# Centring first: a transposed copy without the deviation for two pairs of tiles, and one queue for the first loads

## The chip, the cores and the metric

The kernel runs on one core of a Trainium2 chip. The metric is the device time of one execution in microseconds (us). The kernel before takes 153.9 us (median of 3 runs, 153.81 to 154.15). The profiled execution, from which all durations below come, took 153.96 us, of which 152.2 us lie between its first and its last instruction.

## The reference

x is 2048 x 448 (bf16). Each row is normalised, and two branches and x itself are added up:

```
xn  = (x - mean) / sqrt(var + eps)
q, k, v = xn @ wqkv                      # 16 heads of 28
pq, pk  = q @ w_phi, k @ w_phi           # one 28 x 28 matrix for each head
phi     = [softmax(p), softmax(-p)]      # for pq and pk, 56 features
kv, z   = sum over s of phi_k * v, of phi_k
o       = (phi_q @ kv) / (phi_q @ z + 1e-6)
h       = xn @ w1 + b1                   # 448 -> 1792
out     = x + o @ wo + (h * tanh(softplus(h))) @ w2
```

Normalising a row is a subtraction and a product with one number, rstd = 1/sqrt(var + eps). Products with a matrix are linear, so xn @ W = rstd * ((x - mean) @ W), row by row.

## The kernel before, in words

The 2048 rows are 16 tiles t of 128 rows; two tiles make a pair u = t // 2. A pair's normalised rows (xn, 2 x 448 wide) are turned (transposed) into xnT, seven chunks of 128 features. The odd 64 features of the two tiles share the middle chunk, which is why most products run as two halves of 64 rows that TensorE (PE) executes at once; 14 such halves make one step for a pair.

The order is written out by hand in one string, ORDER (L147). Each word is a step, and each engine gets its instructions in the order in which the steps stand there. The words, with u, t or fc (one of 14 columns of 128 of w1) as number:

- `lx`: load of x tiles; `lkm`, `lkt`, `lvm`: the key and value columns of wqkv, rows 0 to 383 and the last 64 rows, loaded twice, into partitions 0 to 63 and 64 to 127; `lqT`: the query columns by a transposing DMA; `l1m`, `l1t`: w1. The last letter is the queue (s for SP, a for ACT).
- `z12`: twelve products of zeros on PE at the start. `st`: mean and variance of a tile (on DVE, or on ACT by two sums). `rs`, `rt`: rstd (on POOL, or on ACT by Ln and Exp). `xn`: normalising. `xt`: turning a pair, by PE and copies out of PSUM (b, a, d) or by a transposing DMA on SP's queue (m).
- `wtk0`, `wtk1`, `wmk0`, `wmk1`: the key columns are turned on PE, copied to SBUF, multiplied by w_phi and copied into Wpk, so that pk = xn @ Wpk in one step. `qd`, `wmq0`, `wmq1`: the same for queries, from the four `lqT` loads, into Wpq.
- `v`, `k`, `q` with A, B, H: the three parts of a pair's step (14 halves) for values, keys and queries. Then ACT or DVE copies the values (L509, L511), and ACT writes exp(+p) and exp(-p), one instruction of 896 columns for each sign over both tiles (L609, L682).
- `kn`, `kc`: sum of the key exponentials over a head (DVE), reciprocal, product (POOL, L621 or L633). `kv`: the sum over s (L650), which needs all of these. `e`: the query exponentials turned by DMA. `nd`: numerator and denominator (L723). `f`: h for half of the rows and one fc, then ACT's Mish (L703). `wo`, `g`: the two output products (L845, L828). `sto`, `stt`: stores.

PSUM has eight banks; v, k, q and f each take a pair of banks and give it back when the last copy or activation out of it has run. The pair taken is the one that was used longest ago, so PE can be at most four such steps ahead of the engine that empties them.

Waits are put down once the order is fixed: each instruction waits for the last writers and readers of what it touches.

Of the kernel before, what the change touches and what calls it, by code (L numbers as in the profile page):

```python
# [146 lines left out]
ORDER = """  # L147
pi lx1.2a pw table lx0.1s lx4.6a lx2.4a zero st1d lpa st5a st0d st4d st2d rs0p lvma rs2p lx6.8a xn0a xn1d lkms xn5p
lkts xn4p lx8.10s lbs st3d z12 wtk0a rt2a wtk1d xt0b lqT3 rt3a wmk0d wmk1a pp b1 xt2b xn2d st8d lqT1 lqT2 lqT0 xn3d
st9d k0B lx12.14a k2B xt1m st7d qd lx10.12s lx14.16a rt8p pv st6d k0A k0H st12d rt9p k2H v2Ba v0Ba v2Ha v2Aa v0Aa rs3p  # L150
st13d xn6d l1ts st15d xn7d xt3m v0Ha wmq1a wmq0a k2A rt12p rt13p xn13p xn12p st10d xt6m xn8p st14d k1A v1Bd k1B st11d
q2B k1H rs5p v1Ad q1H q2H v1Hd rt14a q1B xn10d q2A xn9d xn14d rt15p pk xt4m q0A q1A q0B k3B xn15d xt7m v6Ba k3H q0H
v6Aa xn11p kn0.1 k6H v6Ha k3A kn0.0 xt5m kn1.1 l1ms k6A v3Ad kc3 k6B v3Hd k7A v3Bd k7H v4Hd kn6.0 e3 v4Ad k7B v4Bd k4B
v7Ba k4H k4A e2 k5B kn7.1 v7Aa kn7.0 q4H k5A v7Ha kc2 e0 k5H q4A e5 f0.0B q4B f0.0H v5Bd f0.0A e9 f0.8H f0.8A v5Ad
kn5.0 f0.3B f0.8B v5Hd f0.3A e1 f0.4B f0.3H e8 q3B f0.4A f0.5A f0.4H f0.5H f0.2H f0.2A kn1.0 f0.5B kn4.1 q5H e4 q5A
f0.2B q3H kn6.1 loa q7B q5B q7A q7H kn5.1 kn4.0 kv2 kv6 ep kv1 kv0 kv5 kv7 kv4 kv3 q3A f1.0B kvz f0.9A e10 f1.0A f1.0H
e14 f0.9H e15 f0.6A f0.9B f0.7B f0.6H nd0 f0.7A f0.6B f0.11H f0.11A f0.7H f0.10B nd3 f0.11B f0.12A f0.10A e11 e6
f0.10H nd1 f0.12H e7 ot0m f0.1B f0.12B f0.1A f0.1H q6A q6H f1.13H nd2 q6B f1.5A f1.13A f1.4A f1.13B f1.5H f1.1H f1.1A
f1.4B f1.1B f1.5B f1.6A f1.6H e12 f1.4H ot1m f1.11A f1.6B f1.11B nd4 f1.12H f1.11H l2s f1.12A f0.13B f1.12B f1.7A nd5
f1.7H f0.13H f0.13A f1.2H f1.7B ot2m f1.2A nd7 wo0H f1.2B wo1B wo0A wo1A nd6 ot3m wo1H wo0B nd10 g2 g7 g3 g1 g0 nd12  # L160
e13 f1.10A f1.10H f1.9A f1.9H wo3B f1.10B nd13 f1.9B wo3A wo3H f1.8B ot6m f1.3H nd11 f1.3A ot5m g6 g5 f1.8H nd15 f1.8A
wo2H f1.3B sto1 wo2B nd14 nd9 wo2A nd8 g4 sto3 g14 g9 sto2 g12 ot7m g8 ot4m g13 wo7H wo4B wo7A wo5A wo6A wo5H wo6H
wo4A wob wo5B wo4H wo6B wo7B sto0 g10 g11 g15 sto6 stt14 sto5 sto4 stt15
"""
# [815 lines left out]
```

## Time and profile before

| | |
|---|---|
| median of 3 runs | 153.9 us |
| profiled execution | 153.96 us |
| its span, first to last instruction | 152.2 us |
| outside the span | 1.76 us |
| PE busy | 144.6 us (95%) |
| DVE busy | 101.1 us (66%) |
| ACT busy | 75.7 us (50%) |
| POOL busy | 44.3 us (29%) |

A row of the timeline or of the chain begins with its start and its length in us. A row of the groups gives the count, the busy time, the mean length of one in ns, and the idle time before. Back-to-back instructions of one engine overlap by their ends, so n of them take less than n times the mean length; the time from one start to the next is what a queue of them costs.

### The profile page before, as it was taken

The page shows a single profiled execution, that of the slowest core. Times are in us where ns is not written, and L with a number is a line of the kernel's source. Part 1 is how long each engine was busy: PE and PEld are TensorE (multiplying, and loading weights), DVE is VectorE, ACT ScalarE, POOL GpSimd, SP SyncE. Part 2 cuts the span into 40 slices and gives each one's busy share as a digit, 9 for nine tenths or more (in the row PEclk, how much of TensorE's full clock was granted, in tenths as well). Part 3 has the DMA queues.
Part 4 walks back from the last instruction along what each step waited for, and adds up shares of the span by engine and source line. Part 5 has one row for each costly group of instructions (what it writes and reads, how often), then busy time and mean ns, then how long its engine had stood idle before and what let it go on. Part 6 is the DMA issues. An engine that isn't in the chain of part 4 may idle for free.

```text
span 152.2 us, 3611 instructions
## 1 busy us (share of the span) xinstructions
PE 144.6 (95%) x1541; PEld 76.1 (50%) x1541; DVE 101.1 (66%) x223; ACT 75.7 (50%) x90; POOL 44.3 (29%) x65
## 2 busy tenths in 40 slices
PE   3978999989999979999999999999999999999993
PEld 1454545445444574445344455554544554559552
DVE  0699989599969903599606999535995999200721
ACT  3485999995995699778997730000500400000000
POOL 3385688969999950000000000000000000000000
PEclk9999999999999999999999999999999999999999
DMA  5995964989967243994399260500035000540204
GB/s 123 288 260 147 174 143 93 131 268 262 101 137 138 76 139 73 180 197 41 60 149 321 86 65 14 119 0 0 2 65 151 30 4 0 121 121 4 87 4 151
DMA packets 40436, 17.22 MB, mean 113 GB/s; under 512 B 34020, under 2 KB 39908, under 8 KB 40420
## 3 DMA queue, kind: packets, MB, share of 16 engines
q1 hardware_dynamic: 37548, 14.46, 46.9%
q10 hardware_dynamic: 2872, 2.53, 5.6%
q8 instruction: 12, 0.20, 0.5%
q14 instruction: 4, 0.03, 0.1%
HBM read 7.02 MB, written 1.84 MB: 58 GB/s over the span
## 4 chain that ended last, share of the span: by engine, by line
PE 78%; ACT 12%; DMA 4%; DVE 3%; issue 1%; ACTq 0%
PE PS L429 38%; PE PS L828 28%; PE PS L845 7%; DMA x_all<-in_A_x_dram 4%; ACT actT L609 3%; PE PS L723 2%; PE PS L650 2%; ACT actT L682 2%; ACT v_all L509 2%; DVE Sk L627 1%; ACT Wpq L509 1%; ACT Eq L682 1%; DVE v_all L511 1%; ACT Eq L509 1%; ACT Wpk L509 1%
## 5 line engine op out<-in xcount | busy, mean ns | idle before, releaser
L703 ACT ACTIVATE actT<-PS,b1T 128x1024 bf16<-128x1024 f32 x28 | 30.2, 1112 | 33.1 <-PE PS L429 33.0
L429 PE MATMUL PS<-xnT,W 64*128 64x512 bf16 x392 | 46.2, 376 | 0.0
L828 PE MATMUL PS<-W,actT 128*128 128x448 bf16 (+1 forms) x224 | 42.7, 351 | 0.0
L828 PEld LDWEIGHTS PS<-W,actT 128*128 128x128 bf16 x224 | 21.5, 98 | 20.3 <-issue 0.7
L429 PEld LDWEIGHTS PS<-xnT,W 64*128 64x128 bf16 x392 | 18.1, 94 | 21.0 <-ACT actT L703 0.4
L793 DVE TENSOR_TENSOR x_all<-PS,x_all 128x448 bf16<-128x448 f32 (+1 forms) x16 | 9.5, 616 | 20.3 <-PE PS L845 10.3
L621 POOL TENSOR_TENSOR actT<-actT,rSk 128x896 bf16<-128x896 bf16 x12 | 20.0, 1699 | 0.0
L609 ACT ACTIVATE actT<-PS 128x896 bf16<-128x896 f32 x16 | 13.7, 950 | 3.7 <-DVE stats L466 1.8
L429 PE MATMUL PS<-Wkv,xnT 64*128 64x448 bf16 x112 | 13.6, 349 | 0.6 <-DVE v_all L511 0.6
L429 PE MATMUL PS<-Wpk,xnT 64*128 64x448 bf16 x112 | 13.3, 349 | 0.5 <-ACT Wpk L509 0.5
L429 PE MATMUL PS<-Wpq,xnT 64*128 64x448 bf16 x112 | 12.7, 350 | 0.0
L466 DVE BATCH_NORM_STATS2 stats<-x_all 128x6 f32<-128x448 bf16 x15 | 9.2, 614 | 5.2 <-DMA x_all<-in_A_x_dram 5.2
L617 DVE TENSOR_REDUCE Sk<-actT 128x32 f32<-128x896 bf16 x12 | 12.5, 1043 | 0.0
L738 DVE COPY Sq<-PS 128x16 f32<-128x16 f32 x32 | 4.0, 167 | 12.5 <-PE PS L723 12.2
L749 DVE TENSOR_TENSOR xn<-v_all,rden 128x448 bf16<-128x448 f32 x16 | 10.0, 625 | 1.3 <-DMA Wkv<-xn 0.8
L746 DVE TENSOR_TENSOR v_all<-v_all 128x464 f32<-128x464 f32 x16 | 10.3, 642 | 0.6
L742 DVE TENSOR_TENSOR v_all<-PS,Sq 128x464 f32<-128x464 f32 x16 | 10.3, 642 | 0.5
L744 DVE TENSOR_TENSOR v_all<-PS,Sq 128x464 f32<-128x464 f32 x16 | 10.1, 630 | 0.0
L429 PEld LDWEIGHTS PS<-Wkv,xnT 64*128 64x128 bf16 x112 | 5.4, 94 | 6.0 <-DVE v_all L511 1.0
L682 ACT ACTIVATE actT<-PS 128x896 bf16<-128x896 f32 x10 | 8.4, 926 | 0.0
L429 PEld LDWEIGHTS PS<-Wpk,xnT 64*128 64x128 bf16 x112 | 5.3, 94 | 5.5 <-ACT Wpk L509 0.6
L429 PEld LDWEIGHTS PS<-Wpq,xnT 64*128 64x128 bf16 x112 | 5.1, 94 | 5.4 <-ACT actT L609 0.5
(85 smaller groups left out, 137.7 us busy)
## 6 DMA issues: line engine op xcount, KB each, us to landing
W<-in_B_w_dram SPq DMA_DIRECT2D x1, 1568.0 KB, 8.0
out_dram<-x_all SPq DMA_DIRECT2D x7, 224.0 KB, 2.2
W<-in_B_w_dram SPq DMA_DIRECT2D x1, 1344.0 KB, 7.2
x_all<-in_A_x_dram ACTq DMA_DIRECT2D x5, 224.0 KB, 4.1
Wo<-in_A_wo_dram ACTq DMA_DIRECT2D x2, 336.0 KB, 3.6
x_all<-in_A_x_dram SPq DMA_DIRECT2D x2, 224.0 KB, 4.9
W<-in_B_w_dram SPq DMA_DIRECT2D x2, 224.0 KB, 4.0
Wkv<-in_A_wqkv_dram SPq DMA_DIRECT2D x1, 336.0 KB, 4.2
```

What stands on the lines that cost most here:

```text
L429: ins = e.matmul(o, lhs(c, k), rhs(c, k), start=first and n == at[par][0], stop=last and n == at[par][-1])
L609: op("ACT", lambda e, s=s: e.activation(E_of(u)[:, s, :, :], two(b, D), ACT.Exp, scale=1.0 if s == 0 else -1.0), r=[pb(b), pb(b + 1)], w=[ ...
L617: op("DVE", lambda e: e.tensor_reduce(Sk[u][:, s, :], Eh(), AX.X, ALU.add), r=[("E", u, s)], w=[("Sk", u, s)], tag=f"Sk{u}.{s}")
L621: op("POOL", lambda e: e.tensor_tensor(Eh(), Eh(), ap_on(rSk[u][:, s, 0:1], [[1, 2 * H], [0, DH]]), ALU.mult), r=[("E", u, s), ("rSk", u, ...
L682: op("ACT", lambda e, s=s: e.activation(Eq_of(u)[:, :, s, :].rearrange("p i (h n) -> p i h n", n=64)[:, :, :, 0:QP], two(b, D).rearrange(" ...
L703: op("ACT", lambda e: e.activation(actT[:, q, fc, :], bank(b, 2), ACT.Mish, bias=b1T[:, fc:fc + 1]), r=[("b1T",), pb(b), pb(b + 1)], w=[(" ...
L742: op("DVE", lambda e: e.tensor_tensor(tv(t1[i]), num(0), sx(1), ALU.mult), r=[pb(b), pb(b + 1), ("Sq", i, 1)], w=[("t1", i)], tag=f"ta{t}")
L744: op("DVE", lambda e: e.tensor_tensor(tv(t2), num(1), sx(0), ALU.mult), r=[pb(b), pb(b + 1), ("Sq", i, 0)], w=[("t2",)], tag=f"tb{t}")
L746: op("DVE", lambda e: e.tensor_tensor(t1[i], t1[i], t2, ALU.add), r=[("t1", i), ("t2",)], w=[("t1", i)], tag=f"tc{t}")
L749: op("DVE", lambda e: e.tensor_tensor(o_sb[(t // 2) % 2][:, t % 2, :].rearrange("p (h d) -> p h d", d=DH), t1[i][:, :, 0:DH], ap_on(rden[i ...
L828: ins = e.matmul(bank(b)[:, 0:width(t)], act_of(fc, t), W2[:, fc, 0:width(t)], start=first and fc == 0, stop=last and fc == FC - 1)
L845: ins = e.matmul(bank(b)[:, 0:w], oT_of(u)[lo:hi, cc * P:(cc + 1) * P], Wo[lo:hi, cc, 0:w], start=first and n == at[par][0], stop=last and ...
```

## The change

For two pairs (u = 0 and u = 2) the turned copy is made of x - mean, before rstd is known. It lies in the space of EqT, which is free at that time. `xc` centres a tile (DVE or POOL), `ct` turns the pair on PE, with one ACT copy of 896 columns out of PSUM. The v, k and q steps of these pairs read this copy, and rstd goes in where the results leave PSUM: as the per-partition scale of a copy (values) or of Exp (keys, queries; nrstd = -rstd for the second sign). rstd differs between the two tiles of a pair, so each such instruction covers one tile, 448 columns. The same two pairs are still normalised and turned the old way (by DMA) for the f steps. The last 64 rows of the key columns are loaded once, and the four transposes that read them run as two halves each. All loads of the first stage go through SP's queue, w_phi and b1 through ACT's. `z12` is `z7`. The whole ORDER string is another.

```diff
-pi lx1.2a pw table lx0.1s lx4.6a lx2.4a zero st1d lpa st5a st0d st4d st2d rs0p lvma rs2p lx6.8a xn0a xn1d lkms xn5p
...
+lx1.2s zero pw lx0.1s lx4.6s st1d lkms xc1d lkts pi pp table lpa lx2.4s st0a xc0d lba st5d rt1p lvts xc5p st4d z7 rt0a
...
+    nrstd = sb("nrstd", [P, 8], FP32)
...
+    XR, XC = (15, 14, 13, 12), (11, 10, 9, 8)
+
+    def flat_of(t):
+        return EqT[:, t, :, :].rearrange("p c n -> p (c n)")[:, 0:7 * P]
+
+    def xR(u):
+        return flat_of(XR[u]).rearrange("p (c n) -> p c n", n=P)
...
+    def load_kv_tail(i, eng):
+        lo, hi = HALF[i]
+        dst, src = (Wv, A_wqkv[384:448, 2 * D:3 * D]) if i else (Wkv, A_wqkv[384:448, D:3 * D])
+        dma(eng, lambda e: e.dma_start(dst[lo:hi, 3, :], src), w=[("Wt", i)], tag=f"ldWt{i}")
...
-                    ins = e.transpose(oT(c)[:, g, :], Wk[:, 2 * h + c, g * GP:(g + 1) * GP], ident[:])
+                    for lo, hi in HALF if h and c else ((0, P),):
+                        ins = e.transpose(oT(c)[:, g, lo:hi], Wk[0:hi - lo, 2 * h + c, g * GP:(g + 1) * GP],
+                                          ident[0:hi - lo, 0:hi - lo])
...
+    def center(t, eng):
+        u = t // 2
+        for n, (lo, hi, at) in enumerate([(0, D, 0)] if t % 2 == 0 else [(384, D, D), (0, 384, D + 64)]):
+            src, dst = x_all[:, t, lo:hi], flat_of(XC[u])[:, at:at + hi - lo]
+            op(eng, lambda e, src=src, dst=dst: e.tensor_scalar(dst, src, mv[:, t, 0:1], 0.0, op0=ALU.subtract, op1=ALU.add),
+               r=[("x", t), ("mean", t)], w=[("xc", u, t % 2, n), ("EqT", XC[u])], tag=f"xc{t}.{n}")
...
+        pe(lambda e: transpose7(e, b, flat_of(XC[u])), r, [pb(b)], f"cT{u}")
+        evac(eng, lambda: flat_of(XR[u]), lambda: bank16(b)[:, 0:7 * P], [pb(b)], [("xR", u), ("xRU", u)] + home, f"cTE{u}")
...
+    def v_early(u, part, eng):
...
+                if eng == "ACT":
+                    op("ACT", lambda e, dst=dst, src=src, t=t: e.mul(dst, src, rstd[:, t:t + 1]), r=r, w=w, tag=f"vs{u}.{i}")
...
+    def k_early(u, part):
+        def then(b):
+            for s in range(2):
+                for i in range(2):
+                    t = 2 * u + i
+                    op("ACT", lambda e, s=s, i=i, t=t: e.activation(E_of(u)[:, s, i, :], bank(b + i)[:, 0:D], ACT.Exp,
+                                                                    scale=sign_rstd(t, s)),
...
+    def q_early(u, part):
```

On PE, the start of the program, before (L504 turns normalised pairs, L547 and L571 are the key columns' `wtk` and `wmk`, L429 the v, k, q steps):

```order
L370 MATMUL PS<-zeros 128x512 x12
L547 MATMUL PS<-ident,Wkv 112x128 x16
L504 MATMUL PS<-ident,xn 128x128 x7
L571 MATMUL PS<-Wbd,Eq 128x112 x16
L695 MATMUL PS<-ident,b_rows 128x14
L504 MATMUL PS<-ident,xn 128x128 x7
L429 MATMUL PS<-Wpk,xnT 128x448 x22
L429 MATMUL PS<-Wkv,xnT 128x448 x28
L571 MATMUL PS<-Wbd,WqT 128x112 x16
```

Now (the lines have moved: L524, L568, L593, L449):

```order
L390 MATMUL PS<-zeros 128x512 x7
L524 MATMUL PS<-ident,EqT 128x128 x7
L568 MATMUL PS<-ident,Wkv 112x128 x12
L568 MATMUL PS<-ident,Wkv 112x64 x8
L593 MATMUL PS<-Wbd,Eq 128x112 x16
L786 MATMUL PS<-ident,b_rows 128x14
L524 MATMUL PS<-ident,EqT 128x128 x7
L449 MATMUL PS<-Wkv,EqT 128x448 x6
L449 MATMUL PS<-Wpk,EqT 128x448 x6
```

The first pair is turned ahead of the key columns, from the centred copy, and the first v half-step stands ahead of the first k half-step.

On ACT, from the first turned pair on, before (L509 copies out of PSUM, L609 key exponentials):

```order
L509 ACTIVATE xnT<-PS 128x384
L478 ACTIVATE lnv<-mv,eps_col 128x1
L480 ACTIVATE rstd<-lnv 128x1
L509 ACTIVATE Wpk<-PS 128x896
L509 ACTIVATE xnT<-PS 128x384
L273 DMA x_all<-in_A_x_dram 128x896 x2
L609 ACTIVATE actT<-PS 128x896 x2
L509 ACTIVATE v_all<-PS 128x32x28 x2
L509 ACTIVATE Wpq<-PS 128x2x4x56 x4
L609 ACTIVATE actT<-PS 128x896 x4
```

Now (L529 copies, L662 values with rstd, L673 key exponentials with rstd or -rstd):

```order
L529 ACTIVATE EqT<-PS 128x896
L529 ACTIVATE Wpk<-PS 128x896 x2
L529 ACTIVATE EqT<-PS 128x896
L498 ACTIVATE lnv<-mv,eps_col 128x1
L500 ACTIVATE rstd<-lnv 128x1
L515 ACTIVATE xn<-x_all,shift,rstd 128x448
L662 ACTIVATE v_all<-PS,rstd 128x16x28 x2
L673 ACTIVATE actT<-PS,rstd 128x448 x2
L673 ACTIVATE actT<-PS,nrstd 128x448 x2
L498 ACTIVATE lnv<-mv,eps_col 128x1
L500 ACTIVATE rstd<-lnv 128x1
L529 ACTIVATE Wpq<-PS 128x2x4x56 x2
```

ACT copies both turned pairs and both halves of Wpk whole, and has four instructions of 448 columns where a key step had two of 896.

On SP's queue, the first loads, before:

```order
L273 DMA x_all<-in_A_x_dram 128x448
L276 DMA Wkv<-in_A_wqkv_dram 128x3x448
L281 DMA Wkv<-in_A_wqkv_dram 64x896 x2
L273 DMA x_all<-in_A_x_dram 128x896
L303 DMA b_rows<-in_B_b_dram 14x128
L285 DMA_TRANSPOSE WqT<-in_A_wqkv_dram 128x448 x4
L516 DMA_TRANSPOSE xnT<-xn 128x7x128
L273 DMA x_all<-in_A_x_dram 128x896
L281 DMA W<-in_B_w_dram 64x1792 x2
```

Now:

```order
L287 DMA x_all<-in_A_x_dram 128x448 x2
L287 DMA x_all<-in_A_x_dram 128x896
L290 DMA Wkv<-in_A_wqkv_dram 128x3x448
L301 DMA Wkv<-in_A_wqkv_dram 64x896
L287 DMA x_all<-in_A_x_dram 128x896
L301 DMA Wkv<-in_A_wqkv_dram 64x448
L290 DMA Wkv<-in_A_wqkv_dram 128x3x448
L287 DMA x_all<-in_A_x_dram 128x896 x2
L304 DMA_TRANSPOSE WqT<-in_A_wqkv_dram 128x448 x4
L536 DMA_TRANSPOSE xnT<-xn 128x7x128
L287 DMA x_all<-in_A_x_dram 128x896
L287 DMA x_all<-in_A_x_dram 128x1792
```

Five loads that stood in ACT's queue now stand ahead of the transposing loads for the queries, and the last two loads of x stand behind the first transposed pair, which waits for DVE.

More of the change, by code (lines that the diff above doesn't have):

```diff
@@ L153 @@
[L153 to L162, printed above, removed]
@@ L244, in _kernel, with early_of @@
                  "Wp1": [("Wp", 1, h, c) for h in range(2) for c in range(2)]}
+    XR, XC = (15, 14, 13, 12), (11, 10, 9, 8)
[3 more added lines that the diff above has]
+        return flat_of(XR[u]).rearrange("p (c n) -> p c n", n=P)
+    def early_of(t):
+        return [(n, XR.index(t)) for n in ("xR", "xRU")] if t in XR else \
+            [("xc", XC.index(t), i, n) for i in range(2) for n in range(2 if i else 1)] if t in XC else []
     def oT_of(u):
@@ L292, in rows_of @@
     def rows_of(name):
-        return [(name, 0), ("Wt", 0), ("Wt", 1)] if name in ("Wk", "Wv") else [(name, i) for i in range(3)]
+        return [(name, 0), ("Wt", 0)] + ([("Wt", 1)] if name == "Wv" else []) if name in ("Wk", "Wv") else \
+            [(name, i) for i in range(3)]
     def load_phi(eng):
@@ new lines, in k_early, with then @@
+    def k_early(u, part):
+        def then(b):
+            for s in range(2):
+                for i in range(2):
+                    t = 2 * u + i
+                    op("ACT", lambda e, s=s, i=i, t=t: e.activation(E_of(u)[:, s, i, :], bank(b + i)[:, 0:D], ACT.Exp,
+                                                                    scale=sign_rstd(t, s)),
+                       r=[pb(b + i), ("rstd", t), ("nr", u)], w=[("E", u, s)] if i else [("Eh", u, s)], tag=f"exkc{u}.{s}.{i}")
+        pair_part(f"k{u}", part, tok_works(u, Wp[1], True),
+                  x_res(u, True) + [("Wp", 1, h, c) for h in range(2) for c in range(2)], then)
@@ new lines, in q_early, with then @@
+    def q_early(u, part):
+        def then(b):
+            for s in range(2):
+                for i in range(2):
+                    t = 2 * u + i
+                    op("ACT", lambda e, s=s, i=i, t=t: e.activation(
+                        Eq_of(u)[:, i, s, :].rearrange("p (h n) -> p h n", n=64)[:, :, 0:QP],
+                        bank(b + i)[:, 0:D].rearrange("p (h n) -> p h n", n=QP), ACT.Exp, scale=sign_rstd(t, s)),
+                       r=[pb(b + i), ("Eqp", u % 3), ("rstd", t), ("nr", u)], w=[("Eq", u % 3, s)],
+                       tag=f"exqc{u}.{s}.{i}")
+        pair_part(f"q{u}", part, tok_works(u, Wp[0], True), x_res(u, True) + [("Wp", 0, c) for c in range(4)], then)
@@ L903, in _kernel @@
                 add(f"f{q}.{fc}{part}", ffn1, q, fc, part)
+    for u in range(4):
+        add(f"nr{u}", minus_rstd, u)
+        for eng, c in (("ACT", "a"), ("DVE", "d"), ("both", "b")):
+            add(f"ct{u}{c}", center_T, u, eng)
+        for part in "ABH":
+            add(f"v{u}{part}e", v_early, u, part, "ACT")
+            add(f"v{u}{part}f", v_early, u, part, "DVE")
+            add(f"k{u}{part}c", k_early, u, part)
+            add(f"q{u}{part}c", q_early, u, part)
+        for t in (2 * u, 2 * u + 1):
+            add(f"xc{t}d", center, t, "DVE")
+            add(f"xc{t}p", center, t, "POOL")
     add("kvz", kvz)
```

62 lines of the change are left out of this document (50 added, 12 removed).

## The prediction

> **What bounds the kernel now.** I read the page first, then the chain of waits, busy time by stretches of the span, and the timeline of the first 60 us.
>
> ```profile
> span 152.2 us, 3611 instructions
> PE 144.6 (95%) x1541; PEld 76.1 (50%) x1541; DVE 101.1 (66%) x223; ACT 75.7 (50%) x90; POOL 44.3 (29%) x65
> ...
> GB/s 123 288 260 147 174 143 93 131 268 262 101 137 138 76 139 73 180 197 41 60 149 321 86 65 14 119 0 0 2 65 151 30 4 0 121 121 4 87 4 151
> ...
> 11.92 4.17 PE PS L429 x42
> ...
> 56.10 0.78 issue
> ...
> 149.83 0.19 DVE x_all L814
> ...
> 11.90:34.20 22.30, 21.70 (x232) 11.18 (x232) 19.52 (x49) 19.80 (x28) 17.50 (x31) 1.00 0.83 163
> 34.20:57.20 23.00, 22.21 (x314) 12.11 (x316) 17.63 (x25) 17.83 (x20) 21.02 (x15) 1.00 0.71 142
> 57.20:91.00 33.80, 33.80 (x445) 16.19 (x444) 22.19 (x54) 27.25 (x26) 0.01 (x1) 1.00 0.68 132
> ```
>
> PE is the bound. From 57 us on it never stands still (33.80 of 33.80), and behind its end come only a sum of 0.19 us and a store. So the change can win or lose in three places: before 11.92 us, where the dense products begin; in the gaps up to 57 us; and inside the key-value sum (0.78 us in which PE waits for nothing that the profile shows). In the first two stretches ACT is busy for 19.80 and 17.83 us, 89% and 78%: it empties PSUM, and is the next bound there. PE's amount of work is the same in both kernels, so I ask at which time the new order has got how far.
>
> **Start: what removes the wait.** These rows carry it.
>
> ```profile
> 3.63 0.63 DVE L466 BATCH_NORM_STATS2 stats<-x_all 128x6 f32<-128x448 bf16 x1 [3.63 <-DMA x_all<-in_A_x_dram]
> 5.42 0.58 ACT L458 ACTIVATE junk<-x_all 128x448 bf16<-128x448 bf16 x1 [2.87 <-DMA x_all<-in_A_x_dram]
> 7.25 0.63 DVE L466 BATCH_NORM_STATS2 stats<-x_all 128x6 f32<-128x448 bf16 x1 [0.99 <-DMA x_all<-in_A_x_dram]
> 9.44 0.66 DVE L511 COPY Eq<-PS 112x1024 bf16<-112x1024 bf16 x1
> 10.96 0.90 ACT L509 ACTIVATE Wpk<-PS 128x896 bf16<-128x896 f32 x1
> 11.92 2.25 PE L429 MATMUL PS<-Wpk,xnT 64*128 64x448 bf16 x22 [0.45 <-ACT Wpk L509]
> ...
> L467 DVE BATCH_NORM_AGGREGATE mv<-stats 128x2 f32<-128x6 f32 x15 | 2.7, 182 | 0.5
> L492 DVE TENSOR_SCALAR xn<-x_all,mv,rstd 128x448 bf16<-128x448 bf16 x4 | 1.5, 382 | 0.0
> L498 POOL TENSOR_SCALAR xn<-x_all,rstd,shift 128x448 bf16<-128x448 bf16 x3 | 2.2, 725 | 0.0
> x_all<-in_A_x_dram SPq DMA_DIRECT2D x1, 112.0 KB, 2.6
> ```
>
> The centring has no row. It is a tensor-scalar of the same shape as the normalising; I take 0.38 us a tile on DVE and 0.73 on POOL (a tile cut in two some 0.6 and 1.1); bounds: nothing, and twice that, 0.4 us more for a pair. By hand: x1, first in its queue, lands at 3.6 as now; statistics 3.6 to 4.4; centring x1 to 5.0, x0 (mean by ACT's sum, 0.7 us from about 3.9) to 5.4. PE turns the pair, then both halves of the key columns (which land by about 5.5 on the same count: 0.92 MB). DVE has two more statistics to make, so its copies of the turned key columns (0.66 each) run 7.0 to 8.3; the two products with w_phi end at 8.35 and 9.0; ACT copies Wpk 8.4 to 10.1. The first v half-step needs none of this, only the turned pair and Wv (eighth of ten loads; 1.55 MB are through by then, at 123 GB/s for the first 3.8 us and 288 after it by the page's row: 7.5 us): it starts at 9.4, the first k half-step at 10.1. So PE is dense 2.5 us earlier than 11.92, with a hole of 0.25.
>
> **What it adds on ACT.** A queue's price for one activation is the time from one start to the next.
>
> ```profile
> 8.17 0.76 ACT L495 ACTIVATE xn<-x_all,shift,rstd 128x448 bf16<-128x448 bf16 x1 [1.06 <-DVE shift L486]
> 17.72 1.86 ACT L509 ACTIVATE Wpq<-PS 128x448 bf16<-128x448 f32 x4
> 22.61 0.38 ACT L478 ACTIVATE lnv<-mv,eps_col 128x1 f32<-128x1 f32 x1
> 23.17 3.35 ACT L682 ACTIVATE actT<-PS 128x896 bf16<-128x896 f32 x4
> 43.30 2.12 ACT L703 ACTIVATE actT<-PS,b1T 128x1024 bf16<-128x1024 f32 x2
> ...
> L509 ACT ACTIVATE Wpq<-PS 128x448 bf16<-128x448 f32 x4 | 1.9, 568 | 0.0
> L682 ACT ACTIVATE Eq<-PS 128x896 bf16<-128x896 f32 x4 | 3.5, 926 | 0.1
> L703 ACT ACTIVATE actT<-PS,b1T 128x1024 bf16<-128x1024 f32 x6 | 6.6, 1113 | 2.1 <-PE PS L429 2.1
> ```
>
> The 896-column exponentials step by (3.35 - 0.93)/3 = 0.81, the 448-column copies by (1.86 - 0.57)/3 = 0.43, so a column costs 0.84 ns and the fixed part 0.05. Mish, the one with a per-partition column as operand, steps by 2.12 - 1.11 = 1.01 where 1024 columns should step by 0.91: the column costs 0.10. An Exp of 448 columns with rstd as scale should therefore step by 0.43 + 0.10 = 0.53; bounds 0.43 (the column is hidden) and 0.66 (nothing overlaps). Four make 2.1 us, where a step had two of 0.81, 1.6: 0.5 more for each of k0, k2, q2, q0, and 0.25 for v0's two copies. The Trainium skill (ScalarE: Activation LUTs, What ACT_TABLE_LOAD costs) says that a pointer operand adds about 93 ns and that neighbours overlap by 93 ns; the Mish row agrees with the first, 0.10, and the sum by the page's figure would be the same.
>
> ACT's queue from 8.4 us on: three copies of 896 (2.4), two pairs of Ln and Exp for rstd and two more later (0.55 each, by the row at 22.61 and its successor at 23.17), one normalised tile (0.65), v0 (1.05), k0 (2.1), half of Wpq (0.85), k2 (2.1), k1, q1, v1 (4.0), q2, q0 (4.2), k3, v5, k5 (4.0): it is at 32.2 us when k5 is done, if nothing makes it wait. PE waits for it: the queries' weights stand behind v0's copy and k0's exponentials on PE's queue. PE is through with v0, k0, v2, k2 at 14.1, and stands until 14.9 (the query columns, doubled by DVE) and 15.4 (k0's last exponential); k1 starts at 16.8, when the first half of Wpq is out.
>
> ```profile
> 17.65 1.31 PE L429 MATMUL PS<-Wpk,xnT 64*128 64x448 bf16 x12
> 14.01 2.81 PE L429 MATMUL PS<-Wkv,xnT 64*128 64x448 bf16 x28
> 72.20 8.79 PE L429 MATMUL PS<-xnT,W 64*128 64x512 bf16 x80
> 15.01 0.23 DVE L289 COPY WqT<-WqT 128x256 bf16<-128x256 bf16 x1
> ```
>
> Before, with the same work done, k1 started in the 17.65 row's second half, at 18.2. So of 2.5 us 1.4 are left. Then ACT sets the pace: with four pairs of banks, q2's rest waits for k2 (19.4), q0 for k1 (21.5), k3 for q1 (23.1), v5 for q2 (26.1), k5 for q0 (28.2), k4 for k3 (29.8). From there the two hand over to each other: k4 is complete at 32.8, ACT (idle for 0.8) takes it to 34.6, k6 waits for k7's exponentials (37.1), the fourth f half-step for k6's (42.0), and PE is through with it at 42.9. A pair of halves costs 0.19 us for 448 columns (28 halves in 2.81 us) and 0.216 for 512 (80 in 8.79); by these the old kernel had done as much at 43.7. The lead is down to 0.8 us.
>
> **Key-value sum: where some of it comes back.** Before, PE gets there at 52.87. POOL's products for it end at 55.0, and near the end of the 128 short products PE stands for 0.78 us, put down to issue.
>
> ```profile
> 45.03 9.99 POOL L621 TENSOR_TENSOR actT<-actT,rSk 128x896 bf16<-128x896 bf16 x6
> 52.87 3.24 PE L650 MATMUL PS<-actT,v_all 128*60 128x112 bf16 x124
> 56.88 0.29 PE L650 MATMUL PS<-actT,v_all 128*60 128x112 bf16 x4 [0.78 <-issue]
> ```
>
> Now POOL's sixteen products (1.67 us each in a queue) start when k2 has its sums and xn15, xn12 are out of the way, at 27.5; with xn13 between them they end at 55.7. PE reaches the sum at 53.5 (five Mish results and q3 stand between; by my count the banks come free for all but 1.5 us of it). The sum's own time is 57.17 - 52.87 - 0.78 = 3.5; POOL's last pair also stands last on PE, so PE need not wait for it. The 0.78 is the open price: between nothing and 0.78, and as the same 128 products stand in one piece again, I take it whole: the end is 57.7. The new order has done more by then: q3's last part (0.56) and, of f steps, 6.71 instead of 6, at 1.51 each: 1.63 us. The old kernel would be there at 57.17 + 1.63 = 58.8. Lead: 1.1 us. Behind that the chain is PE alone in both, and I find no new wait in it: KVZ is turned by 62, its first reader is due at 62.8, and the last loads and stores keep their distance.
>
> Single load of the key tail: 0.1 MB less, under other loads; eight half transposes for four, beside DVE's statistics: nothing. All in one queue: w1 comes late.
>
> ```profile
> 28.93 0.58 SPq L276 DMA_DIRECT2D W<-in_B_w_dram  x1
> 38.38 0.81 PE L429 MATMUL PS<-xnT,W 64*128 64x512 bf16 x6
> ...
> W<-in_B_w_dram SPq DMA_DIRECT2D x1, 1344.0 KB, 7.2
> ```
>
> It is issued behind the last turned pair, at 31.6, lands 7.2 later at 38.8, and is read at 40.7: nothing, with a cover of 1.9 us.
>
> **Sum.** 153.96 - 1.1 = 152.9 for a profiled execution, which stood 0.06 above the median of the runs: 152.8 us.
>
> **Rivals.** *Dear activations* (other side): in the stretch from 13 to 28 us ACT is the pace, and 18 activations take the new form. If each steps by 0.66 instead of 0.53, that is 18 x 0.13 = 2.3 us later on PE: 155.1. For it: no row has this form, and the normalising on ACT with two columns took 0.76 for 448. Against: everything else on ACT overlaps. It decides from a step of 0.59, where the 1.1 us are gone. Chance 0.15.
>
> *Cold start*: PE's speed.
>
> ```profile
> 0.81 0.10 POOL L325 MEMSET mhalf<- 128x4 f32 x1 [0.29 <-POOLq L965]
> 2.15 0.10 POOL L322 MEMSET zeros<- 128x2 bf16 x1
> 2.31 5.03 PE L370 MATMUL PS<-zeros 128*128 128x512 bf16 x12 [2.31 <-POOL zeros L322]
> ```
>
> The twelve products of zeros start 0.43 us apart (12 in 5.03), those of 512 columns later 0.216: PE runs at half speed in the first 7 us, though the page's clock row shows full clock. The Trainium skill (TensorE: Matmul & The Clock Gate, Part 1) says that it takes a window of about 3.4 us of sustained work to get the full rate, and that idle time takes it away. Now the zeros are set first on POOL, where L325 stood at 0.81, and seven products, from 1.0 to 4.0 us, are followed by 1.4 us of nothing. If PE is still at half speed at 9.4, turning and products cost 0.5 us more up to Wpk, and the first 1.5 us of dense work lose 0.75: a delay of ACT's queue by 0.8 to 1.4, 153.9. Chance 0.2.
>
> *Late queue*: SP's order holds x8 to x15 and w1 behind turned pairs that wait for DVE and POOL. If xn13 is 3 us late, w1 is read at 41.8, and the f steps, with all behind, lose 1.1: 153.9. Chance 0.1.
>
> *Cheap activations*: a step of 0.43 gives 18 x 0.1 = 1.8 us on ACT. POOL's last product at 55.7 and one pair behind it (3.5/8) end the sum at 56.2 at the earliest, so PE can use 1.5 of it: 151.3. Chance 0.15.
>
> **How the numbers follow.** Forecast 0.4, the rivals 0.6 as told. Runs of this kernel differ by about 0.2% (0.3 us), so "faster" means under 153.6 and "slower" over 154.2. The forecast is faster but for 0.02, cheap activations are, and of the cold start and the late queue, which are worked out for their larger price, a third each: 0.38 + 0.15 + 0.1 = 0.63. Slower: dear activations, and a third of those two, 0.25. Within: 0.12. The range reaches from the cheap activations, 151.3, to just under the dear ones, 154.9. The forecast's own range is 152.0 (no gap in the sum) to 153.6.
>
> **What would show it.** The first dense L449 row at 9.2 to 9.7; L673's four stepping by 0.53; k1's row at 16.8; PE idle around L593's second group, about 1.2 us in all; the L741 rows from about 53.5 to 57.7 with the gap inside. I am wrong if PE still steps by 0.43 for 512 columns (0.37 a pair of 448) past 9 us, if ACT's four take 2.6 us or more, or if PE waits for w1.

## The result and the profile after

The changed kernel takes 155.54 us (median of 5 runs, 155.01 to 155.87) where the kernel before takes 153.92 us beside it (5 runs, 153.81 to 154.22). The ratio is 1.0106, with a 95% interval of 1.0086 to 1.0125: slower by 1.6 us, and outside the predicted range. The profiled execution took 155.54 us, with a span of 153.8. In all that follows medians are over all runs, and ratios leave out the runs that are over 1.5% longer than the shortest of their kernel (three of e8_z9, one each of e7_dve_only and e11_before_zero_first).

The page of the changed kernel, its first part, and in a second fence the busy time by stretches (PE, PEld, DVE, ACT, POOL, with their counts; then PE's clock, the share of the DMA engines, GB/s). The first stretch begins at 9.00, where the prediction wanted the dense products to begin, in place of 11.90:

```profile
span 153.8 us, 3641 instructions
PE 147.0 (96%) x1540; PEld 77.2 (50%) x1540; DVE 100.2 (65%) x223; ACT 79.4 (52%) x103; POOL 48.8 (32%) x71
```

```profile
9.00:34.20 25.20, 23.82 (x240) 12.44 (x242) 21.91 (x60) 22.87 (x42) 19.33 (x38) 1.00 0.89 154
34.20:60.00 25.80, 25.80 (x354) 14.27 (x352) 17.75 (x24) 23.68 (x26) 23.32 (x16) 1.00 0.70 143
60.00:91.00 31.00, 30.54 (x380) 14.74 (x378) 19.20 (x48) 23.36 (x22) 0.23 (x1) 1.00 0.68 145
```

PE stands for 1.38 us in the first stretch, for nothing in the second, for 0.46 in the third; in the kernel before it stood for 0.60, 0.79 and 0.01 in stretches that correspond roughly. So waiting explains little of the lost time. PE is busy for 147.0 us against 144.6, with five products of zeros fewer and nothing added but four small transposes, cut in two. If the busy time of PE grows without more work, its products take longer. PE's timeline shows where (start, length, then line, shapes and count):

```profile
0.95 3.17 PE L390 MATMUL PS<-zeros 128*128 128x512 bf16 x7 [0.95 <-POOL zeros L342]
5.13 0.90 PE L524 MATMUL PS<-ident,EqT 128*128 128x128 bf16 x7 [1.01 <-DVE EqT L630]
6.57 2.41 PE L568 MATMUL PS<-ident,Wkv 128*112 128x128 bf16 x20 [0.54 <-DMA Wkv<-in_A_wqkv_dram]
8.91 1.78 PE L593 MATMUL PS<-Wbd,Eq 112*128 112x112 bf16 x16
10.74 0.93 PE L524 MATMUL PS<-ident,EqT 128*128 128x128 bf16 x7
11.60 1.30 PE L449 MATMUL PS<-Wkv,EqT 64*128 64x448 bf16 x6
12.70 1.09 PE L449 MATMUL PS<-Wpk,EqT 64*128 64x448 bf16 x6
14.01 0.73 PE L449 MATMUL PS<-Wkv,EqT 64*128 64x448 bf16 x6
14.58 0.73 PE L449 MATMUL PS<-Wpk,EqT 64*128 64x448 bf16 x6
19.38 0.93 PE L449 MATMUL PS<-Wpk,xnT 64*128 64x448 bf16 x8
56.12 3.34 PE L741 MATMUL PS<-actT,v_all 128*60 128x112 bf16 x128
```

The dense products begin at 11.60, not at 9.4, and the first six halves of 448 columns step by 1.10/3 = 0.37 us a pair (12.70 less 11.60, for three pairs), where the six at 14.01 take 0.57 (14.58 less 14.01), 0.19 a pair. PE runs at half rate to about 13 us. k1 starts at 19.38 (forecast 16.8), and PE comes to the key-value sum at 56.12 (forecast 53.5). Both are 2.6 late: between them the forecast of 36.7 us stands, measured 36.74.

### The profile page after: what moved, and what is told of

It reads as the page before. It is cut to its first block, busy times and chain, and to the rows that moved or that the text cites. A ratio compares the mean times of both kernels' runs of the same rounds, so it can differ in the third digit from the quotient of the medians.

```text
span 153.8 us, 3641 instructions
## 1 busy us (share of the span) xinstructions
PE 147.0 (96%) x1540; PEld 77.2 (50%) x1540; DVE 100.2 (65%) x223; ACT 79.4 (52%) x103; POOL 48.8 (32%) x71
## 4 chain that ended last, share of the span: by engine, by line
PE 57%; ACT 24%; DMA 10%; SPq 5%; issue 2%; DVE 0%; ACTq 0%
PE PS L919 28%; PE PS L449 17%; PE PS L936 7%; DMA EqT<-actT 5%; ACT actT L794 5%; SPq L781 4%; ACT actT L773 3%; DMA Wkv<-in_A_wqkv_dram 3%; ACT actT L673 3%; PE PS L814 2%; DMA KVZ<-KVT 2%; ACT actT L700 2%; ACT Eq L773 2%; ACT L794 2%; PE PS L568 2%
## 5 line engine op out<-in xcount | busy, mean ns | idle before, releaser
L449 PE MATMUL PS<-xnT,W 64*128 64x512 bf16 x392 | 45.1, 376 | 0.1
L449 PEld LDWEIGHTS PS<-xnT,W 64*128 64x128 bf16 x392 | 19.0, 94 | 21.0 <-ACT actT L794 1.4
L712 POOL TENSOR_TENSOR actT<-actT,rSk 128x896 bf16<-128x896 bf16 x10 | 16.8, 1707 | 0.0
L449 PE MATMUL PS<-Wpk,xnT 64*128 64x448 bf16 x84 | 10.2, 350 | 0.8 <-ACT Eq L684 0.8
L700 ACT ACTIVATE actT<-PS 128x896 bf16<-128x896 f32 x12 | 10.4, 935 | 0.7 <-PE PS L449 0.7
L708 DVE TENSOR_REDUCE Sk<-actT 128x32 f32<-128x896 bf16 x10 | 10.4, 1042 | 0.0
L449 PE MATMUL PS<-Wpq,xnT 64*128 64x448 bf16 x84 | 10.3, 349 | 0.0
L449 PE MATMUL PS<-Wkv,xnT 64*128 64x448 bf16 x84 | 10.1, 349 | 0.0
L724 POOL TENSOR_TENSOR actT<-actT,rSk 128x896 bf16<-128x896 bf16 x6 | 10.0, 1709 | 0.0
L814 PEld LDWEIGHTS PS<-KVZ,EqT 56*128 56x128 bf16 x256 | 5.7, 93 | 3.8 <-ACT actT L794 1.0
L718 DVE TENSOR_REDUCE Sk<-actT 128x64 f32<-128x1792 bf16 x3 | 5.9, 1981 | 2.1 <-ACT actT L700 2.1
L518 POOL TENSOR_SCALAR xn<-x_all,rstd,shift 128x64 bf16<-128x64 bf16 (+2 forms) x12 | 6.6, 558 | 1.5 <-DVE shift L506 1.4
```

Source lines behind the costliest of these rows:

```text
L449: ins = e.matmul(o, lhs(c, k), rhs(c, k), start=first and n == at[par][0], stop=last and n == at[par][-1])
L700: op("ACT", lambda e, s=s: e.activation(E_of(u)[:, s, :, :], two(b, D), ACT.Exp, scale=1.0 if s == 0 else -1.0), r=[pb(b), pb(b + 1)], w=[ ...
L708: op("DVE", lambda e: e.tensor_reduce(Sk[u][:, s, :], Eh(), AX.X, ALU.add), r=[("E", u, s)], w=[("Sk", u, s)], tag=f"Sk{u}.{s}")
L712: op("POOL", lambda e: e.tensor_tensor(Eh(), Eh(), ap_on(rSk[u][:, s, 0:1], [[1, 2 * H], [0, DH]]), ALU.mult), r=[("E", u, s), ("rSk", u, ...
L724: op("POOL", lambda e, s=s: e.tensor_tensor(Eh(s), Eh(s), ap_on(rSk[u][:, s, 0:1], [[1, 2 * H], [0, DH]]), ALU.mult), r=[("E", u, s), ("rS ...
```

## The experiments

Each kernel is the changed one or the one before with the edit shown; all medians below are of their own runs, and every ratio is to the kernel before, run beside it (153.86 to 154.0 us).

**Twelve zeros instead of seven.**

```diff
-... lvts xc5p st4d z7 rt0a
+... lvts xc5p st4d z12 rt0a
```

> The changed kernel with twelve products of zeros at the start again, instead of seven; nothing else. Theory C (PE at half speed): in the changed kernel the transposes of the key columns stood 107 ns apart and the first v half-step took 1.30 us instead of 0.73, up to about 13 us. With PE busy from 0.95 to 6.1 us it is at full rate by 7 to 7.5, the products with w_phi end at 9.1 instead of 10.6, the second turning (which waits for POOL's centring, done at 9.87) ends at 10.4, the dense products begin at 10.4 instead of 11.6, k1 at 17.6 to 18.0 instead of 19.4, and the time falls by 1.5 us to 154.0 (153.6 to 154.5). Rival Q (the one queue, or the activations, set the time): no change, 155.5 within 0.3.

Measured: 153.59 us, ratio 0.9975 (0.9959 to 0.9991). Five more products of zeros make the kernel 1.95 us faster than with seven. PE's timeline of this kernel, the same rows:

```profile
0.95 4.15 PE L390 MATMUL PS<-zeros 128*128 128x512 bf16 x12 [0.95 <-POOL zeros L342]
6.43 1.45 PE L568 MATMUL PS<-ident,Wkv 128*112 128x128 bf16 x20 [0.65 <-DMA Wkv<-in_A_wqkv_dram]
7.95 1.28 PE L593 MATMUL PS<-Wbd,Eq 112*128 112x112 bf16 x16
9.83 0.56 PE L524 MATMUL PS<-ident,EqT 128*128 128x128 bf16 x7 [0.49 <-POOL EqT L630]
10.33 0.74 PE L449 MATMUL PS<-Wkv,EqT 64*128 64x448 bf16 x6
17.59 0.93 PE L449 MATMUL PS<-Wpk,xnT 64*128 64x448 bf16 x8
```

Seven take 3.17 us, twelve only 4.15: the last ones already run at the full rate. From there on everything does: the key columns 1.45 for 2.41, w_phi 1.28 for 1.78. Dense products start 1.27 us sooner and k1 1.79 sooner. Only the number of zeros differs, so this is the experiment that shows the cause.

**Seven zeros in the kernel before**, the same edit the other way round.

```diff
-lkts xn4p lx8.10s lbs st3d z12 wtk0a rt2a
+lkts xn4p lx8.10s lbs st3d z7 wtk0a rt2a
```

> The kernel before with seven products of zeros instead of twelve; nothing else. Theory C: the zeros end at 5.3 us, PE stands until the key columns are there at 7.0, and turns them and makes Wpk at half speed: dense products 0.5 us later and the first 1.5 us of them at half speed, 0.8 us in all: 154.7 (154.3 to 155.4). Rival: the old kernel starts its dense products for other reasons (the copies by ACT and DVE) and has room: 153.9 within 0.3.

Measured: 154.55 us (153.97 to 156.12), ratio 1.0063 (1.0033 to 1.0093). The old kernel loses too, but only 0.6 us: its zeros start at 2.31 and run straight into the key columns. PE's rows show one thing more:

```profile
7.57 0.65 PE L547 MATMUL PS<-ident,Wkv 128*112 128x128 bf16 x8 [1.08 <-DMA Wkv<-in_A_wqkv_dram]
9.60 1.61 PE L571 MATMUL PS<-Wbd,Eq 112*128 112x112 bf16 x16 [0.34 <-ACT Eq L509]
```

The second half of the key columns runs at the full rate (eight in 0.65 us), and w_phi's products behind it at the half rate again (1.61, where the kernel before has 0.96). PE had reached the full rate and lost it.

**Two queues for the first loads again**, with seven zeros.

```diff
-lx4.6s  lx2.4s  lvms  lx6.8s
+lx4.6a  lx2.4a  lvma  lx6.8a
```

> The changed kernel (seven products of zeros) with four of the first loads back in ACT's queue: x2 to x5, x6 and x7, and the main part of the value columns. Theory C: PE is at half speed all the same, 155.5 (155.1 to 155.8). Rival Q (one queue delays the key columns, for which PE waited 0.54 us, until 6.57): the key columns land by 5.6, everything up to Wpk comes 0.5 to 0.9 us earlier, 154.6 to 155.0.

Measured: 155.58 us, ratio 1.0101 (1.0072 to 1.013), as the changed kernel. With a slow PE the one queue costs nothing and wins nothing: with two queues PE waits for the key columns until 6.79, with one until 6.57. Here too the full rate was reached and lost: the first turning, at 5.51, takes 0.55 us where the changed kernel has 0.90, but the key columns take 2.07 and w_phi's products 1.78.

**Twelve zeros, and tiles 4 and 5 centred by DVE.** In the changed kernel POOL centres them, and its rows show twice the price that the prediction took. First the changed kernel's timeline of POOL, then its groups (busy us, mean ns of one), with the normalising of 448 columns beside the centring:

```profile
6.05 3.82 POOL L630 TENSOR_SCALAR EqT<-x_all,mv 128x64 bf16<-128x64 bf16 x3 [1.28 <-DVE mv L487]
```

```profile
L630 POOL TENSOR_SCALAR EqT<-x_all,mv 128x448 bf16<-128x448 bf16 x1 | 1.8, 1781 | 0.0
L518 POOL TENSOR_SCALAR xn<-x_all,rstd,shift 128x448 bf16<-128x448 bf16 x2 | 1.4, 716 | 0.3 <-DVE shift L506 0.3
```

```diff
-... xc5p ... z7 ... xc4p
+... xc5d ... z12 ... xc4d
```

> The changed kernel with twelve products of zeros and the second pair centred on DVE instead of POOL, where the three centring instructions took 3.82 us. Theory C with POOL next: the second turning comes at 9.3 instead of 9.9, the dense products begin at 9.5, k1 at 17.0, 0.6 us less than with twelve products alone: 153.4 (152.9 to 154.0). Rival: the second turning has room, or DVE, which gets 1 us of work more ahead of the copies of the turned key columns, passes that on: no better than twelve products alone.

Measured: 153.13 us, ratio 0.9951 (0.9933 to 0.9969). PE's timeline:

```profile
9.76 0.74 PE L449 MATMUL PS<-Wkv,EqT 64*128 64x448 bf16 x6
16.65 0.93 PE L449 MATMUL PS<-Wpk,xnT 64*128 64x448 bf16 x8
53.53 2.94 PE L741 MATMUL PS<-actT,v_all 128*60 128x112 bf16 x112
56.70 0.58 PE L741 MATMUL PS<-actT,v_all 128*60 128x112 bf16 x16 [0.23 <-POOL actT L712]
```

With both prices mended, the kernel does what the prediction said: dense products from 9.76 (9.4), k1 at 16.65 (16.8), PE at the key-value sum at 53.53 (53.5), the sum's end at 57.3 (57.7), the time 153.13 (152.8).

**DVE's centring with seven zeros**, to see whether the two costs are apart.

```diff
-xc5p  xc4p
+xc5d  xc4d
```

> The changed kernel with tiles 4 and 5 centred by DVE instead of POOL, the zeros left at seven products. Theory C (the cold start and POOL's centring are two costs of their own, that add up): 0.46 us less than the changed kernel, 155.1 (154.8 to 155.4). Rival (with the slow PE in front of it, POOL's centring is hidden, since the pair is not turned until 10.7 us anyway): no change, 155.5. Third (DVE's centring brings PE's work closer together, so PE warms up sooner): under 154.5.

Measured: 155.37 us, ratio 1.0068 (1.0038 to 1.0097). This lies between the first theory and its rival, and the interval reaches into the changed kernel's own (1.0086 to 1.0125): it does not tell them apart. The median speaks against the third. In the profiled run, which is the longest (157.06 us), PE is still slow at 14.89, where six halves take 1.11 us. But two of the twelve runs, 153.67 and 153.93, are under its 154.5, and how fast PE was in those is not known.

**Nine zeros** on the kernel with DVE's centring.

```diff
-z12
+z9
```

> The kernel of e4_z12_dve with nine products of zeros instead of twelve. In e4_z12_dve twelve take 4.92 us, in the changed kernel seven take 3.17 (0.43 each, all at the slow rate), so nine should end at about 4.8 with 0.3 to 0.9 us of nothing before the first turning. Theory C (PE needs over 3 us of work without a break, and the seven just miss it): nine are enough or nearly so, the pair of tiles is turned at the full rate, 153.1 to 153.6. Rival (what counts is that no idle time stands before the first turning): nine leave PE slow to about 12 us, 154.6 to 155.1.

Measured: 153.95 us, ratio 0.9975 (0.9948 to 1.0002), but its single runs go from 152.78 to 156.00, where those of e4_z12_dve stay between 152.74 and 153.47. Neither expectation is right as a whole: nine are sometimes enough. The profiled execution is one where they were, with dense products from 9.66:

```profile
0.95 4.02 PE L390 MATMUL PS<-zeros 128*128 128x512 bf16 x9 [0.95 <-POOL zeros L342]
```

Nine lie at the edge; the five runs of the changed kernel, with seven, are all at 155.0 or more. That PE was slow in the long runs of this kernel is likely, but no profile shows one of them.

**Zeros set first in the kernel before**, twelve as it had.

```diff
-pi lx1.2a pw table lx0.1s lx4.6a lx2.4a zero st1d
+zero pi lx1.2a pw table lx0.1s lx4.6a lx2.4a st1d
```

> The kernel before with its zeros set first on POOL, as in the changed kernel; twelve products as it had. They then start at about 1.0 instead of 2.31 and end by about 5.2, before the first key columns land. Theory C (what e4_z12_dve wins over the kernel before comes from the centred tiles and not from earlier zeros): no gain, 153.9 to 154.2. Rival (an earlier warm PE is itself worth some of the 0.8 us): 153.3 to 153.7. Third (the idle time between the zeros' end and the key columns makes PE slow again): 154.5 or more.

Measured: 153.98 us (153.23 to 155.54), ratio 1.0015 (0.9992 to 1.0038). In the profiled run (154.05 us) everything from the key columns on runs at the full rate, and the dense products begin at 11.79 for 11.92. So earlier zeros alone win nothing that can be measured, and what e4_z12_dve wins over the kernel before is, by what is left, the new order with its centred tiles. Four of the twelve runs are at 154.6 or more, where the third expectation has a PE that grew slow again; no profile shows those.

**Key-value sum turned ahead of tile 6's queries.** In the changed kernel SP's queue has a transpose of the queries in front of the one of the key-value sum, and PE stands for it:

```profile
60.10 1.94 SPq L781 DMA_TRANSPOSE EqT<-Eq  x1
62.09 1.39 SPq L759 DMA_TRANSPOSE KVZ<-KVT  x1
...
65.78 0.40 PE L814 MATMUL PS<-KVZ,EqT 56*128 56x60 bf16 x16 [0.37 <-DMA KVZ<-KVT]
```

```diff
-kn1.1 kv4 kv0 e6 kv7 kv3 kv2 kv5 kv1 kvz f1.13H
+kn1.1 kv4 kv0 kv7 kv3 kv2 kv5 kv1 kvz e6 f1.13H
```

> The kernel of e4_z12_dve (153.13 us), with the turning of tile 6's queries (eT6, 1.3 us on SP's queue) moved behind the turning of the key-value sum, so that KVZ no longer waits for it: in e4_z12_dve eT6 runs at 58.54 and kvT at 59.90, and the first reader of KVZ stands for 0.21 us at 63.44. Theory C (the rest of the time lost behind the key-value sum is this queue's): KVZ lands some 1.3 us sooner, the 0.21 us are gone, 152.9 (152.7 to 153.1). Rival (the stand is covered by Mish, whose results PE waits for next anyway): no wait at L814, the time unchanged at 153.1.

Measured: 153.35 us, ratio 0.995 (0.993 to 0.9971), on the base of e4_z12_dve with 0.9951. The wait is gone (first reader at 62.84, with no idle time ahead of it), and no time is won that can be measured, as the rival had it.

```profile
56.98 6.02 PE L449 MATMUL PS<-xnT,W 64*128 64x512 bf16 x54
62.84 0.39 PE L814 MATMUL PS<-KVZ,EqT 56*128 56x60 bf16 x16
```

**The rstd column taken out of the early exponentials**, which makes them one instruction of 896 columns a sign, as before the change.

```diff
-    for s in range(2):
-        for i in range(2):
-            op("ACT", ... activation(E_of(u)[:, s, i, :], bank(b + i)[:, 0:D], ACT.Exp, scale=sign_rstd(t, s)))
+    for s in range(2):
+        op("ACT", ... activation(E_of(u)[:, s, :, :], two(b, D), ACT.Exp, scale=1.0 if s == 0 else -1.0))
```

> The kernel of e4_z12_dve with the exponentials of the four early half-steps k0, k2, q0, q2 as one instruction of 896 columns for each sign, with 1 or -1 as scale in place of the rstd column; so rstd is left out of the keys and queries of the first four tiles, and nothing else changes. A step's exponentials then take two of 0.81 us instead of four of 0.52, which is 0.46 us less, 1.8 us in all on ACT before 28 us. Theory C (ACT sets the pace there, and what PE gains is capped at the end of POOL's key products, as the rival of cheap activations was worked out): the key-value sum ends 0.8 to 1.1 us sooner, 152.2 (151.9 to 152.6). Rival (PE is held by other things there, such as DVE's copies and normalising): under 0.3 us, 152.9 to 153.1.

Measured: 153.14 us, ratio 0.9954 (0.993 to 0.9979): the same time as with the column. ACT's timeline of e4_z12_dve (both signs of k0, then the first exponentials behind the four early steps), and ACT's and PE's of this kernel:

```profile
13.11 1.16 ACT L673 ACTIVATE actT<-PS,rstd 128x448 bf16<-128x448 f32 x2
14.14 1.17 ACT L673 ACTIVATE actT<-PS,nrstd 128x448 bf16<-128x448 f32 x2
27.54 1.82 ACT L700 ACTIVATE actT<-PS 128x896 bf16<-128x896 f32 x2
```

```profile
13.05 1.72 ACT L671 ACTIVATE actT<-PS 128x896 bf16<-128x896 f32 x2
26.10 1.73 ACT L695 ACTIVATE actT<-PS 128x896 bf16<-128x896 f32 x2
...
29.14 0.74 PE L449 MATMUL PS<-Wpk,xnT 64*128 64x448 bf16 x6 [0.81 <-DMA xnT<-xn]
43.88 3.68 PE L449 MATMUL PS<-xnT,W 64*128 64x512 bf16 x30 [0.30 <-ACT actT L768]
```

ACT is 1.44 us ahead (26.10 against 27.54). PE then stands 0.81 us for a turned pair, and 0.30 for Mish, and reaches the key-value sum at 53.43, 0.10 sooner. Cheaper activations, a rival with 151.3, win nothing here. (This kernel leaves rstd out of the keys and queries of four tiles; it is there for the time alone.)

**One small DVE instruction moved.** DVE's timeline of e4_z12_dve shows an instruction of one column that takes 4.87 us, and POOL's what comes of it:

```profile
48.61 4.87 DVE L382 SCALAR_TENSOR_TENSOR epsT<-epsT 128x1 f32<-128x1 f32 x1
53.40 1.07 DVE L708 TENSOR_REDUCE Sk<-actT 128x32 f32<-128x896 bf16 x1
...
48.45 5.01 POOL L712 TENSOR_TENSOR actT<-actT,rSk 128x896 bf16<-128x896 bf16 x3
54.94 1.70 POOL L712 TENSOR_TENSOR actT<-actT,rSk 128x896 bf16<-128x896 bf16 x1 [1.48 <-DVE rSk L710]
```

It ends when POOL's three products end. Behind it on DVE stands the last key sum, which POOL's last product and the last pair of the key-value sum wait for. The instruction is not needed until the key-value sum is copied out, so it can move; the base is the kernel of e5_kvt_first.

```diff
-... e15 e11 ep kv6 kn1.1 kv4 ...
+... e15 e11 kv6 kn1.1 ep kv4 ...
```

> The kernel of e5_kvt_first (eT6 behind kvT), and the small sums of the denominator's epsilon (L379, L382) moved on DVE behind the last key sum kn1.1. In e4_z12_dve the one-column L382 holds DVE for 4.87 us, from 48.61 until POOL's three products end at 53.46, so the last key sum is made at 53.40, POOL stands for 1.48 us and its last product ends at 56.6; in e5_kvt_first the same line took 1.41. Theory D (that stall sets the end of the key-value sum when it comes in its long form): POOL's last product follows the one before it directly, no wait for POOL inside the L741 rows, the sum ends at about 56.8 for 57.3, 152.8 (152.5 to 153.1). Rival (the long form comes back on DVE behind kn1.1 and nothing else waits; the end of the sum is PE's own arrival at 53.5 plus 3.3): the same row, but no time won, 153.1 to 153.4.

Measured: 152.54 us (152.06 to 152.87), ratio 0.9916 (0.989 to 0.9943). This is what theory D expected: POOL's last four products are one piece, and so are the L741 rows, from 53.73 to 57.07. POOL of this kernel:

```profile
48.65 6.66 POOL L712 TENSOR_TENSOR actT<-actT,rSk 128x896 bf16<-128x896 bf16 x4
```

The profiled run of e5_kvt_first had the same piece of four already, with L382 at 1.41 us, and was with 152.54 the shortest of its ten runs, four of which are at 152.87 or less; with the edit all six are. The two intervals overlap a little, so the gain of 0.8 us is likely rather than certain. Of the kernels here that compute the reference this is the fastest: 0.84% under the kernel before.

**Both at once**: the edits of e6_wide_exp and e9_eps_late.

> The same two moves on top of e6_wide_exp (rstd left out of the keys and queries of the first four tiles). In e6_wide_exp the 1.8 us taken from ACT brought k4 forward by about 1.4 us on ACT and the first f half-step by 0.75 us on PE, but the median did not move; its L382 took 5.07 us. Theory C (the gain of cheaper activations is real and was lost to POOL's end): 152.5 (152.1 to 152.8), at least 0.4 below e9_eps_late. Rival (it is lost in the f half-steps, which wait for Mish on ACT, and PE comes to the key-value sum at 53.4 in both): the same time as e9_eps_late within 0.2.

Measured: 152.45 us, ratio 0.9921 (0.9898 to 0.9943), as the rival had it. Even with POOL out of the way the 1.8 us on ACT are worth nothing. PE's waits of this kernel between k1 and the key-value sum:

```profile
28.88 0.74 PE L449 MATMUL PS<-Wpk,xnT 64*128 64x448 bf16 x6 [0.31 <-DMA xnT<-xn]
43.99 3.68 PE L449 MATMUL PS<-xnT,W 64*128 64x512 bf16 x30 [0.67 <-ACT actT L768]
```

In e9_eps_late PE stands 0.21 us (until 21.53) and 0.77 (until 28.15) for the early activations, 0.98 in all. Here these waits are gone, and others of 0.31 and 0.67 have come, for a turned pair and for Mish: 0.98 again. PE is at the key-value sum at 53.54, for 53.73.

**Why POOL's centring is dear.** The kernel of e1_z12 with another form of the instruction; the two tiles then hold -0.5 x + mean in place of x - mean.

```diff
-tensor_scalar(dst, src, mv[:, t, 0:1], 0.0, op0=ALU.subtract, op1=ALU.add)
+tensor_scalar(dst, src, mhalf[:, 0:1], mv[:, t, 0:1], op0=ALU.mult, op1=ALU.add)   # on POOL
```

> The kernel of e1_z12 (153.59 us: twelve zeros, POOL centring tiles 4 and 5), with POOL's centring put in the form that its normalising has: a product with one column and an addition of another, both from SBUF, in place of subtracting a column and adding the immediate 0.0. The columns are the -0.5 of mhalf and the mean, so these two tiles hold -0.5 x + mean instead of x - mean, for values, keys and queries; the amount of work is the same. In e1_z12 and the changed kernel the 448 columns took 1.78 us on POOL, the normalising takes 0.73. Theory F (the form is dear): 0.7 to 0.8 us for 448, the pair is ready before PE comes to it, 153.1 (152.8 to 153.4), as with DVE's centring. Rival (the place is dear: bf16 columns into EqT while the loads run): 1.5 us or more again, 153.4 to 153.7.

The line's own rows, of e1_z12 and then of this kernel (least, median and largest ns of one, which are those of 64, 384 and 448 columns; then the first and last start, in us):

```profile
L630 POOL TENSOR_SCALAR EqT<-x_all,mv x3: 516/1568/1782, 5.9 to 8.0; 128x64 bf16<-128x64 bf16 x1, 128x384 bf16<-128x384 bf16 x1, 128x448 bf16<-128x448 bf16 x1
```

```profile
L630 POOL TENSOR_SCALAR EqT<-x_all,mhalf,mv x3: 397/665/726, 5.7 to 6.7; 128x64 bf16<-128x64 bf16 x1, 128x384 bf16<-128x384 bf16 x1, 128x448 bf16<-128x448 bf16 x1
```

It is the form: 1782 ns become 726 at the same place, time and shape. Which part of it (the subtraction or the immediate) stays open. k1 starts at 16.60 as in e4_z12_dve. The time does not show it: 153.55 us, ratio 0.9975 (0.9953 to 0.9997), outside the 152.8 to 153.4 that theory F gave, with runs from 152.33 to 154.07. The profiled run is the one of 152.33, and in it L382 took 1.43 us. That the others had the long form of that instruction would explain the spread, but no profile of them shows it.

## Why the prediction was wrong

It forecast 152.8 (151.3 to 154.9) and faster; the kernel is slower, 155.54. The sum fails at its first term and holds, nearly, behind it.

By the times of the experiments, 1.95 us of the miss go with the number of zeros (155.54 to 153.59), 0.46 more with DVE's centring (to 153.13, with intervals that overlap), and 0.33 stay (153.13 against 152.8).

*Start: what removes the wait.* This step failed. Dense products were to begin at 9.4 and begin at 11.60. Two prices in it were wrong.

- **The rate of PE.** The step priced turning and w_phi's products as if PE were warm (at full rate) by then, and put the doubt into the rival "cold start", with 0.8 to 1.4 us and a chance of 0.2. The rival's mechanism is the cause, and the prediction's own sign of being wrong, 0.37 us a pair past 9 us, is what the rows from 11.60 show. But its price was too low: 1.95 us by e1_z12. It gave 0.5 us to the turning and the products up to Wpk; the first dense product is 1.27 later (11.60 against 10.33). It gave 0.75 to the dense work; k1 is another 0.52 later. With the measured price the rival gives 154.75, not 153.9. The chance was the larger fault: seven zeros at 0.43 are 3.0 us of work, followed by 1.4 us of nothing (1.01 as measured); the row of the kernel before (twelve zeros in 5.03 us, and full rate directly behind them) said that five us were enough, and no row said that three were. The Trainium skill (TensorE: Matmul & The Clock Gate, Part 1) has the window in which PE's activity is counted run freely, so that the moment of the switch varies from run to run; the traces agree, with twelve zeros taking from 4.12 to 4.92 us in kernels that begin them at 0.95, and with nine zeros falling on either side.
- **POOL's centring**, taken as 0.73 for a tile and 1.1 for one in two pieces, by the rows of the normalising: 1.83 us for the pair. It takes 3.82. That is the step's own upper bound, twice the price (3.66); the 0.4 us for a pair that it gave this bound falls short of the 1.83 that doubling adds on POOL. In e1_z12 PE waits for it (0.49 us ahead of the pair's turning at 9.83), and k1 comes 0.94 us later than in e4_z12_dve, and 0.6 later than in e5_kvt_first and e9_eps_late (16.98 and 16.99), which centre on DVE too. In the time e1_z12 and e4_z12_dve are 0.46 apart, with intervals that overlap. In the changed kernel itself PE comes to that pair only at 10.74, with POOL through at 9.87: there the slow PE hides it.

*What it adds on ACT.* Right. The step of a 448-column activation with the rstd column was to be 0.53; in the changed kernel the two signs of k0 start 1.04 apart, so 0.52 for one:

```profile
15.83 1.16 ACT L673 ACTIVATE actT<-PS,rstd 128x448 bf16<-128x448 f32 x2
16.87 1.18 ACT L673 ACTIVATE actT<-PS,nrstd 128x448 bf16<-128x448 f32 x2
```

"ACT sets the pace" from k1 on gave 36.7 us to the key-value sum, and 36.74 were measured. But ACT is not the only one to set it: with cheaper activations DMA and Mish take its place, so the rival on these had a wrong idea of what they are worth. Dear activations did not come, and what they would cost was not tried. "PE idle around L593's second group, about 1.2 us in all" fell: 0.40 before it in the changed kernel, and 0.17 and 0.15 in e4_z12_dve.

*Key-value sum.* The gap of 0.78 us, "the open price", taken whole, did not come: 128 products from 56.12 to 59.46 in one piece. That gave 0.86 back: of 2.62 us on arrival 1.76 were left at the sum's end (59.46 against 57.7). In the kernel before with zeros set first the gap was 1.01 us, and with seven zeros there was none; what it is stays open.

*Behind the sum, "I find no new wait in it".* Wrong by about 0.9 us: by the count of f steps the changed kernel was 0.66 behind at 59.46 (58.8 by the old order), and 1.6 at the end of the span. Of it 0.37 is PE's wait for KVZ, which the queue of query transposes on SP held up: it was to be turned by 62, and its first reader, which waits for it, starts at 65.78; of these 3.8 us 1.8 are the sum's lateness. The other half a microsecond is no such wait: e9_eps_late, in which PE never waits for KVZ, loses 0.4 too (1.8 ahead at 56.99 by the same count, 1.4 at the end of the span). That stays open.

*All in one queue: nothing, with a cover of 1.9 us.* Right: w1 is issued at 33.90 (forecast 31.6), PE does not wait for it, and e3_two_queues changes nothing. The rival "late queue" had no part in it.

The sum of what failed: 2.6 late at k1, less 0.86 in the key-value sum, plus 0.9 behind it, is 2.6 us; the forecast was off by 2.74. That the last two cancel is chance.
